# Smaller buffers and fewer streamed bytes in a recurrent attention over memory: casts into the operand tiles, softmax in PSUM, one output buffer

## The chip, the cores and the metric

The kernel runs on one core of a Trainium2 chip, in one launch. The metric is device time in microseconds: the median of several executions. The profile is of one further execution; its times are in microseconds from the start of its span unless marked ns. PE is TensorE (matmuls; PEld its weight loads), DVE is VectorE, ACT is ScalarE, POOL is GpSimd, SP is SyncE, which issues most DMAs.

## The reference, cut to what matters

The output is two results side by side. Part A is a sliding, dilated attention over x (2048 x 640). Part B, which the change touches, is a recurrence over 64 segments of 32 rows. The 8 memory rows that one segment gives are the memory of the next, so segments can't overlap freely.

```python
for s in range(n_seg):                        # 64 segments, seg_len 32, M = 8, H = 32, Dh = 192
    xs = x[:, s * seg_len:(s + 1) * seg_len, :]
    h = jnp.concatenate([mem, xs], axis=1)    # 40 rows of 640
    q, k, v = (jnp.einsum('btd,dhe->bhte', h, W) for W in (Wq, Wk, Wv))
    scores = jnp.where(mask, jnp.einsum('bhqe,bhke->bhqk', q, k) * scale, -1e9)
    o = jnp.einsum('bhqk,bhke->bhqe', softmax(scores), v)
    o = jnp.einsum('bhte,hed->btd', o, Wo)
    mem = o[:, :M, :]
    outs.append(o[:, M:, :])
```

## The kernel before, in words

**Order of the whole.** Part A comes first; while it runs, the weights of part B that stay in SBUF are loaded, and those that don't are copied into DRAM tiles of their own (`copy_streamed`, L347). Then 64 segments follow (`segment`, L695), and at the end one projection over all segments of the rows that no later segment needs (`project_late`, L776).

**Weights.** Each of q, k, v is cut into four groups of heads of five pieces (`dc`), 384 KB each; Wo into 24 pieces of 320 KB. `STREAMED` (L285) names the pieces that are fetched in every segment from their DRAM copy into one of 7 rotating buffers (`fetch`, L434; SP's queue). All others are resident.

**A segment** runs group by group (g = 0 to 3), in an order written out by hand as tokens: `FIRST` for segment 0, `ORDER` (L297) for the others. PE, DVE, ACT and SP execute their instructions in just that order; each engine takes from a token what is its own. The tokens:

- `q.g k.g v.g` (L504): projections, 32-row tiles, into PSUM `acc` (3 buffers). Once in four segments a group's k and v are also made for the 8 late rows of four segments (`ahead`); q's come one segment early (`ql`).
- `e.k1` (L546): the cast of `acc` into an SBUF tile `sb`, on the engine that `EVACUATE` names (S is ACT, V is DVE; the first letter is for `ahead`, the second for the segment's own). `T.k1` (L549): DVE turns `sb` in 32 x 32 blocks into QT or KT (L522), of which there is one each, and POOL fills the 8 late columns from a kept block `Lb` (L538, L541, L554).
- `S.g` (L573): the scores into a PSUM bank (`px`, 4 in all). `sb.g` (L580) scales and masks them into an SBUF tile `t1`, `mx` (L587), `sub` (L591, and ACT's exp, L592), `send` (L596, L597, L606): the rest of the softmax, into P.
- `tp.g` (L613), `PT.g` (L619): P is turned through PE and spread. `ve.g` (L562): v is kept in `Vst`. `mix.g` (L632): P times V into two banks.
- `ot.g` (L638): two copies, on the engines that `HEADS` names, bring the two halves of the mix into OT (L640). POOL then copies the 8 late columns of OT into OL (L641), which has two halves by g, and issues the DMA that stores OL in DRAM as `late_o` (L642). OT is one tile: `out.g` (L660) reads it as PE's weights.
- `part`, `join`: the two sums of groups 0 to 2 are joined. `last` (L682): group 3's share of the output, into Z. It reads the first half of OT in its first 24 matmuls, the second in the other 24.
- `close` (L685): DVE adds Z and `part` into XS (L687), turns it (L482) and copies the 8 memory rows into HX (L690), the operand of the next segment's first projection. POOL issues the DMAs of the output (L692).

Of the kernel before, what the change touches and what calls it, by code (L numbers as in the profile page):

```python
# [7 lines left out]
FP32 = mybir.dt.float32  # L8
# [15 lines left out]
def part_a(ctx, tc, A_x, A_wqkv, A_wo, out, ident, emit_loads):  # L24
# [241 lines left out]
    with tc.manual_schedule(engines={mybir.EngineType.PE, mybir.EngineType.DVE, mybir.EngineType.Activation}):  # L266
# [4 lines left out]
        for b in range(-1, n_blk):  # L271
# [13 lines left out]
STREAMED = {"q": ((), (), (), ()), "k": ((0, 1, 4), (3,), (0, 3, 4), (0, 1, 3)), "v": ((0, 3), (0, 3), (0, 4), (2, 4)),  # L285
            "o": (9, 11, 14, 16, 20, 23)}
SLOT = 1536
RENEW = {0: ("k0", "v2"), 1: ("k1", "v3"), 2: ("k2", "v0"), 3: ("k3", "v1")}
BLOCKS = 18
FIRST = """  # L290
    q.0 e.q0 T.q0 k.0 e.k0 T.k0 q.1 e.q1 k.1 S.0 sb.0 T.q1 e.k1 mx.0 sub.0 T.k1 send.0 q.2 e.q2 v.0 ve.0
    S.1 sb.1 tp.0 PT.0 T.q2 k.2 e.k2 T.k2 mx.1 sub.1 mix.0 ot.0 v.1 ve.1 send.1 S.2 sb.2 out.0.0 out.0.1
# [24 lines left out]
def part_b(ctx, tc, B_x, B_mem0, B_Wq, B_Wk, B_Wv, B_Wo, out, ident, n_seg, pre, nbuf, mid):  # L317
# [26 lines left out]

    copied = {}

    def copy_streamed():  # L347

        for m, g in need:
            for u in pieces(m, g):  # L350
                if streamed(u):
                    copied[u] = dpool.tile([128, unit_cols(u)], BF16, name="wcopy_%s%d_%d" % u)[:]
                    nc.sync.dma_start(two_rows(copied[u], u), unit_src(u))
# [4 lines left out]
    for m, g in need:  # L358
        resident += [u for u in pieces(m, g) if not streamed(u)]
    res, wait = {}, set()  # L360

    def place_resident(pool, units):
        for u in units:
            res[u] = pool.tile([128, unit_cols(u)], BF16, name="wres_%s%d_%d" % u)[:]

    def load_resident(units):
        for u in units:
            nc.sync.dma_start(two_rows(res[u], u), unit_src(u))

    n_pre, used = 0, 0  # L370
    while n_pre < len(resident) and used < pre:
        used += 2 * unit_cols(resident[n_pre])
        n_pre += 1
# [48 lines left out]
    qk_sb = pool("b_qk", bufs=3)  # L422
# [11 lines left out]
    def fetch(u):  # L434
        t = wstream.tile([128, SLOT], BF16, tag="ws")
        nc.sync.dma_start(t[:, 0:unit_cols(u)], copied[u])
        return t[:, 0:unit_cols(u)]

    def get_unit(u):
        if u in fetched:  # L440
            return fetched.pop(u)
        if u in res:
            if u in wait:
                wait.remove(u)
                load_resident([u])
            return res[u]
        return fetch(u)
# [15 lines left out]
    OT = cpool.tile([128, 12, L], BF16, name="OT")  # L463
    OL = cpool.tile([128, 2, M, 12], BF16, name="OL")
# [33 lines left out]
    def columns(w, m, j):  # L498

        if m == "v":  # L500
            return w[:, 384 * j:384 * j + 384].rearrange("p (f n) -> p f n", n=32)
        return w.rearrange("p (f j n) -> p j f n", j=4, n=32)[:, j]

    def project32(Xs, m, g, part=slice(0, 5), ps=None):  # L504

        if ps is None:
            ps = [ps_acc.tile([128, 384], FP32, tag="acc", name=f"acc{n}") for n in range(len(Xs))]
        for dc in range(5)[part]:
            w = get_unit((m, g, dc))
            for n, X in enumerate(Xs):  # L510
                for j in range(4):
                    nc.tensor.matmul(ps[n][32 * j:32 * j + 32].rearrange("p (f n) -> p f n", n=32), lhsT=X[:, dc, :],  # L512
                                     rhs=columns(w, m, j), start=(dc == 0), stop=(dc == 4), tile_position=(0, 32 * j))
        return ps
# [6 lines left out]
    def turn(dst, sb):  # L521
        nc.vector.transpose(dst, sb[:].rearrange("p (f n) -> p f n", n=32))  # L522
# [8 lines left out]
    def turn_late(sb, m, g, s, start):  # L531

        lt = sb[:].rearrange("p (f n) -> p f n", n=32)
        turn(lt, sb)
        for t in range(start, next_start(m, g, start)):
            rows = lt[:, :, M * (t % 4):M * (t % 4) + M]
            if t == s:
                nc.gpsimd.tensor_copy(columns_of(m, 32, L), rows)  # L538
            else:
                late[m, g, t] = free.pop(0)  # L540
                nc.gpsimd.tensor_copy(late[m, g, t][:], rows)  # L541
# [4 lines left out]
    def evacuate(ps, copies):  # L546
        return [to_sb(p, c) for p, c in zip(ps, copies[2 - len(ps):])]

    def turn_and_fill(s, m, g, sbs):  # L549
        if renewed(s, m, g):  # L550
            turn_late(sbs[0], m, g, s, s)
        else:
            b = late.pop((m, g, s))
            nc.gpsimd.tensor_copy(columns_of(m, 32, L), b[:])  # L554
            free.append(b)
        turn(columns_of(m, 0, 32), sbs[-1])
# [21 lines left out]
    def soft_begin(Sps):  # L578
        t1 = one.tile([128, 4, L], FP32, tag="t1")
        nc.vector.scalar_tensor_tensor(out=t1[:], in0=Sps, scalar=scale,  # L580
                                       in1=mask[:].unsqueeze(1).to_broadcast([128, 4, L]),
                                       op0=ALU.mult, op1=ALU.add)
        return t1
# [54 lines left out]
    def keep_mix(s, g, ps, copies):  # L638
        for r, copy in enumerate(copies):
            copy(OT[:, 6 * r:6 * r + 6].rearrange("p c n -> p (c n)"), ps[r][:, 0:6 * L])  # L640
        nc.gpsimd.tensor_copy(OL[:, g % 2].rearrange("p n c -> p c n"), OT[:, :, 32:L])  # L641
        nc.gpsimd.dma_start(late_o[s // 4][:, g, s % 4], OL[:, g % 2].rearrange("p n c -> p (n c)"))  # L642
# [5 lines left out]

    def wide(w, r, gv):
        return w[:, 640 * r:640 * r + 640].rearrange("p (b g c) -> p g b c", b=2, g=2)[:, gv]  # L650

    def project_out(Y, g, pairs=range(6)):
        for a in pairs:
            i = 6 * g + a
            w = get_unit(("o", i, 0))
            for r in range(2):
                c = 2 * a + r
                for gv in range(2):
                    t = 32 * (2 * r + gv)
                    nc.tensor.matmul(Y[t:t + 32].rearrange("p (b c) -> p b c", b=2),  # L660
                                     lhsT=OT[:, slot(c), 0:32], rhs=wide(w, r, gv),
                                     start=(i == 0), stop=(i == 17), tile_position=(0, t))

    def join_begin(Y):
        part = one.tile([128, 4, L], FP32, tag="t1", name="part")[:].rearrange("p a n -> p (a n)")
        for b in range(2):
            S_(part[64 * b:64 * b + 64], Y[64:128, 160 * b:160 * b + 160])
        return part
# [5 lines left out]

    def project_last(Y):
        for a in range(6):
            w = get_unit(("o", 18 + a, 0))
            for r in range(2):
                c = 2 * a + r
                for j in range(4):  # L680
                    n = 640 * r + 160 * j
                    nc.tensor.matmul(Y[32 * j:32 * j + 32], lhsT=OT[:, slot(c), 0:32], rhs=w[:, n:n + 160],  # L682
                                     start=(c == 0), stop=(c == 11), tile_position=(0, 32 * j))

    def close(s, Y, part):  # L685
        Ysb, T = XS[:], Vst[:, 0:160]
        nc.vector.tensor_tensor(Ysb, Y, part, op=ALU.add)  # L687
        if s + 1 < n_seg:
            turn32(T.rearrange("p (k n) -> p k n", n=SEG), Ysb)
            nc.vector.tensor_copy(HX[:, 0, :, 0:M], T.rearrange("p (k n) -> p k n", n=SEG)[:, :, 0:M])  # L690
# [4 lines left out]
    def segment(s):  # L695
# [12 lines left out]
        def step(name, *at):  # L708
# [3 lines left out]
            elif name == "e":  # L712
                m = at[0][0]
                got["sb", m, g] = evacuate(got.pop((m, g)), [engine[c] for c in EVACUATE[at[0]]])
            elif name == "T":
                m = at[0][0]
                turn_and_fill(s, m, g, got.pop(("sb", m, g)))
# [31 lines left out]
            elif name == "join":  # L749
                join_end(got["Y"], got["part"])  # L750
            elif name == "tx":
# [8 lines left out]
            elif name == "close":  # L760
                close(s, got["Z"], got["part"])
            elif name == "Tql":
                if not last:
                    gl = (s + 1) % 4
                    turn_late(got["sbl"], "q", gl, s, s + 1)
# [10 lines left out]
    def project_late():  # L776
# [8 lines left out]
        def add(m, i, w, first, final):  # L785
            for r in range(2):
                c = (2 * i + r) % 12
                for gv in range(2):
                    for j in range(4):
                        nc.tensor.matmul(sums[2 * m + gv][32 * j:32 * j + 32, 0:320], lhsT=O[4 * m + j][:, i // 6, :, slot(c)],  # L790
                                         rhs=w[:, 640 * r + 320 * gv:640 * r + 320 * gv + 320],
                                         start=first and r == 0, stop=final and r == 1, tile_position=(0, 32 * j))

        def store(m):
            rows = res[DEAD[16 + m]][:, 0:640]
            for gv, copy in ((0, S_), (1, V_)):
                copy(rows[:, 320 * gv:320 * gv + 320], sums[2 * m + gv][:, 0:320])
# [118 lines left out]
```

## Time and profile before

| | |
|---|---|
| Median of 3 runs | 1902.7 us (1901.57 to 1906.56) |
| The profiled execution's own time | 1902.95 us |
| Its span | 1901.2 us, 91723 instructions |
| Mean granted PE clock | 0.988 |
| DMA, whole span | 649.28 MB, mean 342 GB/s |

A row of the costliest groups has line, engine and operation, `out<-in` by tile names, shapes, a count, then after the bar the busy time in us, the mean ns of one, and the engine's idle time before them with what ended it. A row of the waits says who stood waiting for whom: us in all, times, the longest. A row of DMA issues ends with the median us from issue to landing. A row of a stretch has for each engine its busy us and count, in the order PE, PEld, DVE, ACT, POOL, then the granted clock, the DMA engines' share of the time and GB/s. In the chain in order of time and in the timeline, the first number is the start and the second how long it took.

### The profile page before, as it was taken

The numbers are of one execution on the slowest core, as the hardware profiler recorded it, in microseconds if no ns is written. First come the engines' busy times: TensorE is split into PE (matmuls) and PEld (weight loads), VectorE is DVE, ScalarE is ACT, GpSimd is POOL, SyncE is SP. The second block draws the span as 40 slices with busy tenths as digits, with TensorE's granted clock in tenths as the row PEclk, the third lists the DMA queues.
The fourth block names the chain that finished last, engine by engine and source line by source line (L and its number), as shares of the span: only waits on it lengthen the run. The fifth ranks groups of instructions, "written<-read, shape, count | busy, mean of one in ns | idle before, by whom it ended". The sixth has DMA issues, their size and how long they took to land.

```text
span 1901.2 us, 91723 instructions
## 1 busy us (share of the span) xinstructions
PE 1655.8 (87%) x39286; PEld 1042.3 (55%) x39286; DVE 1236.2 (65%) x3495; ACT 695.6 (37%) x1806; POOL 690.6 (36%) x1864
## 2 busy tenths in 40 slices
PE   8997898888888888888888888888889888888888
PEld 5565555555555555555555555555555555555558
DVE  4886676676666666676666676666667676666630
ACT  3453343333333333333333333333333333333320
POOL 3001344344433343433434433334444343443420
PEclk9999999999999999999999999999999999999999
DMA  9927999999999999999999999999999999999991
GB/s 328 318 71 254 329 380 361 376 371 371 352 362 356 359 362 354 350 374 348 355 365 352 362 368 336 359 363 369 370 385 372 356 372 348 349 355 342 372 381 52
DMA packets 286356, 649.28 MB, mean 342 GB/s; under 512 B 61140, under 2 KB 76946, under 8 KB 285948
## 3 DMA queue, kind: packets, MB, share of 16 engines
q1 hardware_dynamic: 267036, 630.01, 91.5%
q0 software_dynamic: 18400, 13.08, 2.2%
q8 instruction: 308, 5.05, 1.0%
q14 instruction: 100, 0.82, 0.1%
q10 hardware_dynamic: 512, 0.33, 0.1%
HBM read 629.10 MB, written 23.24 MB: 343 GB/s over the span
## 4 chain that ended last, share of the span: by engine, by line
PE 57%; DMA 26%; DVE 7%; issue 5%; ACT 2%; POOL 1%; SPq 0%; ACTq 0%; POOLq 0%; DVEq 0%
PE acc L512 30%; DMA t<-wcopy_k 10%; DMA t<-wcopy_o 7%; PE Y L660 7%; DMA t<-wcopy_v 7%; PE px L632 5%; PE px L573 4%; PE pq L95 3%; PE px L682 3%; PE px L790 1%; PE px L613 1%; DVE prod L151 1%; PE po L161 1%; ACT OT L640 1%; PE acc L790 1%
## 5 line engine op out<-in xcount | busy, mean ns | idle before, releaser
L512 PEld LDWEIGHTS <-HX 128*32 128x32 bf16 x19380 | 495.1, 97 | 443.8 <-issue 140.3
L512 PE MATMUL acc<-t,HX 128*32 128x384 bf16 x5812 | 434.0, 332 | 55.1 <-DMA t<-wcopy_k 21.1
L512 PE MATMUL acc<-wres_q,HX 128*32 128x384 bf16 x6460 | 331.8, 329 | 79.4 <-DVE HX L690 67.3
L518 ACT CAST sb<-acc 128x384 bf16<-128x384 f32 x484 | 228.2, 476 | 448.3 <-PE acc L512 381.1
L512 PE MATMUL acc<-wres_v,HX 128*32 128x384 bf16 x3876 | 242.7, 330 | 3.8 <-issue 3.8
L641 POOL COPY OL<-OT 128x96 bf16<-128x96 bf16 x256 | 160.9, 629 | 213.4 <-ACT OT L640 147.0
L554 POOL COPY QT<-Lb 128x96 bf16<-128x96 bf16 x252 | 68.8, 273 | 453.6 <-PE px L573 444.4
L562 ACT CAST Vst<-acc 128x384 bf16<-128x384 f32 x256 | 123.7, 483 | 283.2 <-PE px L632 205.4
L660 PE MATMUL Y<-wres_o,OT 128*32 128x320 bf16 x3584 | 203.3, 303 | 22.8 <-ACT OT L640 14.7
L512 PE MATMUL acc<-wres_k,HX 128*32 128x384 bf16 x3232 | 207.7, 331 | 7.7 <-issue 7.4
L522 DVE STREAM_TRANSPOSE QT<-sb 128x384 bf16<-128x384 bf16 x256 | 143.9, 562 | 78.7 <-ACT sb L518 78.7
L640 ACT CAST OT<-px 128x240 bf16<-128x240 f32 x448 | 143.9, 366 | 111.4 <-PE px L632 109.7
L660 PEld LDWEIGHTS <-OT 128*32 128x32 bf16 x4608 | 118.9, 96 | 97.4 <-issue 37.7
L619 DVE TENSOR_TENSOR PT<-px,own 128x320 bf16<-128x320 f32 x256 | 124.8, 487 | 72.5 <-PE px L613 70.7
L642 POOL DMA_DIRECT2D late_o<-OL x256 | 139.4, 545 | 81.5 <-POOL OL L641 74.5
L522 DVE STREAM_TRANSPOSE KT<-sb 128x384 bf16<-128x384 bf16 x256 | 144.4, 564 | 23.4 <-ACT sb L518 21.7
L573 PEld LDWEIGHTS <-QT 64*64 64x64 bf16 (+1 forms) x4096 | 106.8, 109 | 83.8 <-issue 53.2
L592 ACT ACTIVATE t<-t 128x160 f32<-128x160 f32 x256 | 86.4, 338 | 170.4 <-DVE t L591 168.3
L573 PE MATMUL px<-KT,QT 64*64 64x40 bf16 (+1 forms) x4096 | 138.3, 189 | 11.9 <-DVE KT L522 3.9
L692 POOL DMA_DIRECT2D out_dram<-XS x256 | 129.2, 512 | 15.3 <-DVE XS L687 7.9
L518 DVE CAST sb<-acc 128x384 bf16<-128x384 f32 x162 | 87.2, 547 | 58.7 <-PE acc L512 43.1
L632 PE MATMUL px<-PT,Vst 64*128 64x80 bf16 (+1 forms) x2048 | 122.7, 212 | 1.8 <-issue 1.5
(96 smaller groups left out, 2188.3 us busy)
## 6 DMA issues: line engine op xcount, KB each, us to landing
t<-wcopy_k SPq DMA_DIRECT2D x640, 384.0 KB, 6.0
t<-wcopy_v SPq DMA_DIRECT2D x512, 384.0 KB, 6.1
t<-wcopy_o SPq DMA_DIRECT2D x396, 320.0 KB, 5.6
wres_q<-in_B_Wq_dram SPq DMA_DIRECT2D x20, 384.0 KB, 7.8
late_o<-OL POOLq DMA_DIRECT2D x256, 24.0 KB, 5.3
wres_q<-late_o SPq DMA_DIRECT2D x16, 384.0 KB, 7.4
wres_o<-in_B_Wo_dram SPq DMA_DIRECT2D x18, 320.0 KB, 7.2
wres_v<-in_B_Wv_dram SPq DMA_DIRECT2D x12, 384.0 KB, 7.9
```

The lines of the kernel that those rows point to most:

```text
L512: nc.tensor.matmul(ps[n][32 * j:32 * j + 32].rearrange("p (f n) -> p f n", n=32), lhsT=X[:, dc, :], rhs=columns(w, m, j), start=(dc == 0), ...
L518: copy(sb[:], p[:])
L522: nc.vector.transpose(dst, sb[:].rearrange("p (f n) -> p f n", n=32))
L562: S_(Vst[:], ps[-1][:])
L573: nc.tensor.matmul(Sps[64 * h:64 * h + 64, a, :], lhsT=QT[k0:k1, L * f:L * f + 64], rhs=KT[k0:k1, f, :], start=(outer == 0 and a == 0), st ...
L619: nc.vector.tensor_tensor(PT[:], pt.rearrange("p l (h n) -> p (l h) n", h=2)[:, :, 0:L].unsqueeze(2) .to_broadcast([128, 4, 2, L]), own[:] ...
L632: nc.tensor.matmul(ps[r][lo:hi, 2 * L * k:2 * L * k + 2 * L], lhsT=V[64 * r:64 * r + 64, col:col + hi - lo], rhs=PT[64 * r:64 * r + 64, 2 ...
L640: copy(OT[:, 6 * r:6 * r + 6].rearrange("p c n -> p (c n)"), ps[r][:, 0:6 * L])
L641: nc.gpsimd.tensor_copy(OL[:, g % 2].rearrange("p n c -> p c n"), OT[:, :, 32:L])
L642: nc.gpsimd.dma_start(late_o[s // 4][:, g, s % 4], OL[:, g % 2].rearrange("p n c -> p (n c)"))
L660: nc.tensor.matmul(Y[t:t + 32].rearrange("p (b c) -> p b c", b=2), lhsT=OT[:, slot(c), 0:32], rhs=wide(w, r, gv), start=(i == 0), stop=(i ...
L692: nc.gpsimd.dma_start(out2[SEG * s:SEG * s + SEG - M, Dm + 160 * j:Dm + 160 * j + 160], Ysb[32 * j + M:32 * j + SEG])
```

## The change

1. **Streaming.** k, v and o have other streamed pieces, and three pieces (`PARTS`) are streamed in part: a piece is cut into four quarters, the first 2 or 3 are fetched, the others stay resident. Wo's quarters are kept in the column order of its two sums.
2. **Buffers.** `qk_sb` has 1 buffer instead of 3, `t1` is gone, there are 16 kept blocks instead of 18, OT holds 32 columns instead of 40, OL has one half instead of two.
3. **Casts.** `e` casts the segment's own q and k straight into QT and KT; `T` turns them there, in place. Only the `ahead` part still goes through `sb`. For k0 the kept copies come after T.k1.
4. **Softmax** scales, masks, subtracts and takes exp in the scores' PSUM bank.
5. **OT and OL.** After each of the two copies into OT, the same engine copies the late columns from PSUM into OL. POOL only issues the DMA.
6. **The last sum.** join also turns `part` (`turn_part`); close turns Z from PSUM and adds the turned 8 rows into HX, and only then adds the full rows for the output. `part` and its turned form lie in QT and KT, the turned Z in Vst.
7. `ORDER`, `FIRST`, `EVACUATE` and `HEADS` are others; the copy of `ahead` v (LV) moves from ACT to DVE.

The diff, cut to its core:

```diff
-STREAMED = {"q": ((), (), (), ()), "k": ((0, 1, 4), (3,), (0, 3, 4), (0, 1, 3)), "v": ((0, 3), (0, 3), (0, 4), (2, 4)),
-            "o": (9, 11, 14, 16, 20, 23)}
+STREAMED = {"q": ((), (), (), ()), "k": ((0, 4), (0, 3), (1, 4), (0, 2, 3)), "v": ((0, 2, 4), (2, 4), (0, 3), (2, 4)),
+            "o": (4, 10, 13, 15, 21, 23)}
+PARTS = {("o", 10, 0): 3, ("v", 1, 2): 2, ("v", 2, 3): 3}
-BLOCKS = 18
+BLOCKS = 16
 ORDER = """
-    q.0 e.q0 k.0 T.q0 e.k0 T.k0 k.1 q.1 S.0 e.k1 k.2 e.q1 q.2 sb.0 T.k1 T.q1 S.1 e.k2 mx.0 v.0 sub.0
-    send.0 e.q2 T.q2 q.3 tp.0 sb.1 ve.0 v.1 mx.1 T.k2 sub.1 S.2 PT.0 mix.0 send.1 e.q3 tp.1 ve.1 sb.2
-    k.3 ot.0 mx.2 out.0.0 v.2 PT.1 out.0.1 T.q3 sub.2 e.k3 T.k3 send.2 mix.1 S.3 ve.2 v.3 ot.1 sb.3 mx.3
-    sub.3 tp.2 PT.2 out.1.0 out.1.1 mix.2 send.3 tp.3 PT.3 tx ot.2 ve.3 out.2.0 out.2.1 mix.3 part ql
-    ot.3 eql last join close Tql
+    q.0 k.0 e.q0 e.k0 T.q0 T.k0 q.1 k.1 S.0 e.q1 v.0 e.k1 sb.0 mx.0 T.q1 sub.0 T.k1 q.2 ve.0 S.1 send.0
+    sb.1 mx.1 e.q2 sub.1 k.2 e.k2 tp.0 T.q2 PT.0 send.1 v.1 q.3 T.k2 mix.0 ve.1 tp.1 PT.1 S.2 ot.0 sb.2
+    k.3 e.q3 mx.2 T.q3 mix.1 out.0.0 e.k3 out.0.1 sub.2 T.k3 v.2 send.2 tp.2 ot.1 S.3 ve.2 sb.3 v.3 mx.3
+    out.1.0 sub.3 PT.2 mix.2 out.1.1 send.3 tp.3 ve.3 ot.2 out.2.0 out.2.1 PT.3 mix.3 tx part ql ot.3
+    join eql last close Tql
 """
-EVACUATE = {"k0": "VS", "k1": "VV", "k2": "SS", "k3": "SV", "q0": "SS", "q1": "VS", "q2": "SS", "q3": "SS"}
-HEADS = ("SS", "VS", "SS", "SS")
+EVACUATE = {"k0": "SV", "k1": "SS", "k2": "SS", "k3": "VS", "q0": "SV", "q1": "SS", "q2": "SS", "q3": "VS"}
+HEADS = ("VS", "SS", "SV", "SS")
...
-    qk_sb = pool("b_qk", bufs=3)
+    qk_sb = pool("b_qk", bufs=1)
...
-    OT = cpool.tile([128, 12, L], BF16, name="OT")
-    OL = cpool.tile([128, 2, M, 12], BF16, name="OL")
+    OT = cpool.tile([128, 12, 32], BF16, name="OT")
+    OL = cpool.tile([128, M, 12], BF16, name="OL")
...
-    def evacuate(ps, copies):
-        return [to_sb(p, c) for p, c in zip(ps, copies[2 - len(ps):])]
+    def evacuate(m, ps, copies):
+        sb = to_sb(ps[0], copies[0]) if len(ps) > 1 else None
+        copies[1](columns_of(m, 0, 32), ps[-1][:].rearrange("p (f n) -> p f n", n=32))
+        return sb
...
-            S_(LV[g][:], ps[0][:])
+            V_(LV[g][:], ps[0][:])
...
-        t1 = one.tile([128, 4, L], FP32, tag="t1")
-        nc.vector.scalar_tensor_tensor(out=t1[:], in0=Sps, scalar=scale,
+        nc.vector.scalar_tensor_tensor(out=Sps, in0=Sps, scalar=scale,
...
         for r, copy in enumerate(copies):
-            copy(OT[:, 6 * r:6 * r + 6].rearrange("p c n -> p (c n)"), ps[r][:, 0:6 * L])
-        nc.gpsimd.tensor_copy(OL[:, g % 2].rearrange("p n c -> p c n"), OT[:, :, 32:L])
-        nc.gpsimd.dma_start(late_o[s // 4][:, g, s % 4], OL[:, g % 2].rearrange("p n c -> p (n c)"))
+            o = ps[r][:, 0:6 * L].rearrange("p (c n) -> p c n", n=L)
+            copy(OT[:, 6 * r:6 * r + 6], o[:, :, 0:32])
+            copy(OL[:, :, 6 * r:6 * r + 6].rearrange("p n c -> p c n"), o[:, :, 32:L])
+        nc.gpsimd.dma_start(late_o[s // 4][:, g, s % 4], OL[:].rearrange("p n c -> p (n c)"))
...
+    def turn_part(part):
+        partT = KT[:].rearrange("p f n -> p (f n)")[:, 0:320].bitcast(FP32).rearrange("p (k n) -> p k n", n=SEG)
+        turn32(partT, part)
+        return partT
...
-    def close(s, Y, part):
-        Ysb, T = XS[:], Vst[:, 0:160]
+    def close(s, Y, part, partT):
+        Ysb, T = XS[:], Vst[:, 0:320].bitcast(FP32).rearrange("p (k n) -> p k n", n=SEG)
+        if s + 1 < n_seg:
+            turn32(T, Y)
+            nc.vector.tensor_tensor(HX[:, 0, :, 0:M], T[:, :, 0:M], partT[:, :, 0:M], op=ALU.add)
         nc.vector.tensor_tensor(Ysb, Y, part, op=ALU.add)
-        if s + 1 < n_seg:
-            turn32(T.rearrange("p (k n) -> p k n", n=SEG), Ysb)
-            nc.vector.tensor_copy(HX[:, 0, :, 0:M], T.rearrange("p (k n) -> p k n", n=SEG)[:, :, 0:M])
...
             elif name == "T":
                 m = at[0][0]
-                turn_and_fill(s, m, g, got.pop(("sb", m, g)))
+                keep = fill_late(s, m, g, got.pop(("sb", m, g)))
+                turn_in_place(columns_of(m, 0, 32))
```

More of the change, by code (lines that the diff above doesn't have):

```diff
@@ L350, in copy_streamed @@
             for u in pieces(m, g):
-                if streamed(u):
+                if u in PARTS:
+                    copied[u] = dpool.tile([128, stream_cols(u)], BF16, name="wcopy_%s%d_%d" % u)[:]
+                    load_quarters(copied[u], u, range(PARTS[u]))
+                elif streamed(u):
                     copied[u] = dpool.tile([128, unit_cols(u)], BF16, name="wcopy_%s%d_%d" % u)[:]
@@ L358, in part_b @@
     for m, g in need:
-        resident += [u for u in pieces(m, g) if not streamed(u)]
+        resident += [u for u in pieces(m, g) if not streamed(u) or u in PARTS]
     res, wait = {}, set()
@@ L533, in turn_late, with keep, fill_late @@
         lt = sb[:].rearrange("p (f n) -> p f n", n=32)
[L534 to L539, printed above, removed]
+        turn_in_place(lt)
+        rows = lambda t: lt[:, :, M * (t % 4):M * (t % 4) + M]
+        if start == s:
+            nc.gpsimd.tensor_copy(columns_of(m, 32, L), rows(s))
+        def keep():
+            for t in range(max(start, s + 1), next_start(m, g, start)):
                 late[m, g, t] = free.pop(0)
-                nc.gpsimd.tensor_copy(late[m, g, t][:], rows)
+                nc.gpsimd.tensor_copy(late[m, g, t][:], rows(t))
+        return keep
     def project_qk(s, m, g):
         return project32([ahead, main] if renewed(s, m, g) else [main], m, g)
-    def evacuate(ps, copies):
-        return [to_sb(p, c) for p, c in zip(ps, copies[2 - len(ps):])]
[L549 to L556, printed above, removed]
+    def evacuate(m, ps, copies):
+        sb = to_sb(ps[0], copies[0]) if len(ps) > 1 else None
+        copies[1](columns_of(m, 0, 32), ps[-1][:].rearrange("p (f n) -> p f n", n=32))
+        return sb
+    def fill_late(s, m, g, sb):
+        if sb is not None:
+            return turn_late(sb, m, g, s, s)
+        b = late.pop((m, g, s))
+        nc.gpsimd.tensor_copy(columns_of(m, 32, L), b[:])
+        free.append(b)
     def values(s, g):
@@ L660, in project_out @@
                     nc.tensor.matmul(Y[t:t + 32].rearrange("p (b c) -> p b c", b=2),
[L661 removed]
+                                     lhsT=OT[:, slot(c), 0:32], rhs=quarter(w, ("o", i, 0), 2 * r + gv),
                                      start=(i == 0), stop=(i == 17), tile_position=(0, t))
     def join_begin(Y):
[L665 removed]
+        part = QT[:, 0:320].bitcast(FP32)
         for b in range(2):
@@ L750, in step @@
                 join_end(got["Y"], got["part"])
+                got["partT"] = None if last else turn_part(got["part"])
             elif name == "tx":
```

93 lines of the change are left out of this document (63 added, 30 removed).

## The prediction

> **What bounds the kernel now.** I read the page's busy shares first, then the steady part by itself (the stretch from the first to the last hand-over between segments), the hand-over's own rows, and the waits.
>
> ```profile
> PE 1655.8 (87%) x39286; PEld 1042.3 (55%) x39286; DVE 1236.2 (65%) x3495; ACT 695.6 (37%) x1806; POOL 690.6 (36%) x1864
> ...
> PE 57%; DMA 26%; DVE 7%; issue 5%; ACT 2%; POOL 1%; SPq 0%; ACTq 0%; POOLq 0%; DVEq 0%
> ```
> ```profile
> 216.80:1810.50 1593.70, 1390.72 (x34472) 857.22 (x34472) 1074.77 (x3256) 588.84 (x1581) 639.37 (x1735) 0.99 0.99 362
> ```
> ```profile
> L690 DVE COPY HX<-Vst x63: 174/175/582, 216.6 to 1810.3; 128x40 bf16<-128x40 bf16 x63
> ```
> ```profile
> PE acc L512 <- DVE HX L690: 67.3, 63, 1.4
> POOL OL L641 <- DMA late_o<-OL: 63.0, 37, 2.7
> ...
> PE acc L512 <- DMA t<-wcopy_k: 21.1, 45, 1.7
> ...
> PE acc L512 <- DMA t<-wcopy_v: 15.6, 30, 6.4
> ...
> PE Y L660 <- DMA t<-wcopy_o: 11.1, 25, 1.1
> ```
>
> L690 runs once a segment, 63 times from 216.6 to 1810.3: 62 distances of 25.70 us. In that stretch the DMA engines are busy 0.99 of the time at 362 GB/s and PE 1390.72 of 1593.70 us, 22.4 us a segment. So DMA and PE are both near their limits. PE's direct waits for streamed weights are small all the same, 21.1 + 15.6 + 11.1 = 47.8 us, 0.77 a segment: that is all PE can win from fewer bytes as long as the rest of its order stays. The hand-over costs it 67.3/63 = 1.07.
>
> Keep the second wait in mind: today POOL, which nobody waits for, stands 63.0 us for `late_o` transfers, although OL has two halves.
>
> **The bytes.** Streamed a segment before: 10 pieces of k and 8 of v at 384 KB, 6 of o at 320 KB, 8832 KB. After: k 9 x 384; v seven whole, one half (192), one three quarters (288); o five whole and one of 240: 3456 + 3168 + 1840 = 8464 KB. That is 4.2% less, at 0.99 x 25.70 us of DMA time worth 1.06 us if time goes by bytes. PE can take at most its 0.77. The room for it comes from the smaller buffers.
>
> **The hand-over.**
>
> ```profile
> L522 DVE STREAM_TRANSPOSE KT<-sb 128x384 bf16<-128x384 bf16 x256 | 144.4, 564 | 23.4 <-ACT sb L518 21.7
> ...
> L619 DVE TENSOR_TENSOR PT<-px,own 128x320 bf16<-128x320 f32 x256 | 124.8, 487 | 72.5 <-PE px L613 70.7
> ...
> L592 ACT ACTIVATE t<-t 128x160 f32<-128x160 f32 x256 | 86.4, 338 | 170.4 <-DVE t L591 168.3
> ...
> L596 DVE TENSOR_REDUCE sm<-t 128x4 f32<-128x160 f32 x256 | 78.5, 307 | 44.4 <-ACT t L592 40.9
> ...
> L606 DVE TENSOR_TENSOR P<-t,sm 128x128 bf16<-128x128 f32 x256 | 75.5, 295 | 8.8
> ...
> L606 DVE TENSOR_TENSOR P<-t,sm 128x32 bf16<-128x32 f32 x256 | 48.6, 190 | 0.0
> ...
> L597 DVE RECIPROCAL sm<-sm 128x4 f32<-128x4 f32 x256 | 45.5, 178 | 8.8
> ...
> L482 DVE STREAM_TRANSPOSE Vst<-XS 128x160 bf16<-128x160 bf16 x63 | 22.3, 355 | 2.2
> L687 DVE TENSOR_TENSOR XS<-px,part 128x160 bf16<-128x160 f32 x64 | 20.8, 324 | 72.3 <-PE px L682 72.3
> ...
> L126 DVE TENSOR_REDUCE mx<-lg 128x64 f32<-128x512 f32 x8 | 5.5, 691 | 15.1 <-PE lg L118 15.0
> ...
> L137 DVE TENSOR_TENSOR P<-ex,sm 128x512 bf16<-128x512 f32 x8 | 5.5, 691 | 0.3
> ```
>
> Today it is L687, L482, L690: 0.324 + 0.355 + 0.175 = 0.85 us. After: a turn of 160 f32 columns from PSUM and a sum of 40 columns. No f32 turn is in the trace: at least the 0.355 of the bf16 one, at most twice that; the sum 0.18 to 0.32 (L690, L687). So between a gain of 0.3 and a loss of 0.2; I take a gain of 0.2, nearest to a turn at the same columns. The wide sum moves behind the hand-over, and the second turn (of `part`) goes into join, beside `ql` and `last`.
>
> **Softmax in PSUM.** The same instructions with other operands. L126 reads 512 f32 columns from PSUM, L137 as many from SBUF, both 691 ns: I take nothing. No DVE or ACT row here rewrites PSUM at this size; the ends are 0 and a tenth of each 0.31 us step. By the Trainium skill, "VectorE: DVE Perf Modes", section on the TRN2 errata, a PSUM source costs some 62 cycles (65 ns) more per instruction; the two equal rows do not bear that out.
>
> **Cast into QT and KT.** The turns stay (0.56 us), but a cast now writes a tile that the scores of the group before still read, so it waits for them. Between S.0 and S.1 the chain is cast, sb, mx, turn, sub, cast, turn, with five DVE steps (3 x 0.31 + 2 x 0.56) and a cast ahead, about 2.4 us; PE has v.0 and q.2 there, 1.9. In the same way tp.2 waits for sub.2, T.k3 and send.2. I charge 0.5 us a segment in all (0 if POOL and the order hide it, 1.0 if both stand in full).
>
> **OL: one buffer, written by ACT and DVE.** Gone are POOL's 0.63 us copies. Each of the two copies of OT is now followed on its own engine by one into OL, and the DMA that reads OL must have landed before the next group's first copy writes there. What waits is no longer POOL but ACT (ot.0 to ot.3) and DVE (ot.0, ot.2), in the order written out.
>
> ```profile
> t<-wcopy_k SPq DMA_DIRECT2D x640, 384.0 KB, 6.0
> ...
> late_o<-OL POOLq DMA_DIRECT2D x256, 24.0 KB, 5.3
> ```
> ```profile
> DMA to landing us min/median/max: 3.0/5.3/7.8
> ```
> ```profile
> DMA to landing us min/median/max: 2.0/3.8/9.2
> ```
> ```profile
> 745.44 0.55 POOL L642 DMA_DIRECT2D late_o<-OL  x1 [0.30 <-POOL OL L641]
> ```
> ```profile
> 747.41 0.62 ACT L640 CAST OT<-px 128x240 bf16<-128x240 f32 x2 [1.86 <-PE px L632]
> ...
> 748.92 0.59 ACT L667 COPY part<-Y 64x160 f32<-64x160 f32 x2
> 749.53 0.62 ACT L640 CAST OT<-px 128x240 bf16<-128x240 f32 x2
> ```
> ```profile
> 747.83 1.00 PE Y L660 x24
> 748.83 0.47 PE px L632 x16
> 749.30 0.93 PE acc L512 x20
> 750.23 0.86 PE px L682 x48
> ...
> 759.29 0.47 PE px L573 x16
> ...
> 763.21 0.22 PE px L613 x2
> ```
>
> The first landing row is that of `late_o` (3.0 least, 5.3 median), the second that of part A's `ob`, whose least, 2.0, fell where DMA was nearly idle. In the segment shown ot.2 ends at 748.03 and ot.3 starts at 749.53, 1.5 us later. The transfer starts 0.30 us after OL is written and takes L. After its first OT copy (about 0.35) ot.3 would write OL 1.85 us after ot.2's end, but may only at 0.30 + L: a wait of **L - 1.55**, 3.75 us at the median, 1.45 at the least of `late_o`, 0.45 at 2.0. **Behind it on ACT** stands the second half of OT, and for that waits the second half of `last`, which ends the segment. PE's cover is `ql` (0.93) and half of `last` (0.43).
>
> The wait also passes from group to group. With PE's pieces above (a projection 0.93, scores 0.47, mix 0.47, out 1.00, tp 0.22), an OL copy at 0.2 (the bounds are 0.175, L690, and POOL's 0.63 for twice the columns), and t = 0 at the end of mix.0:
>
> - ot.0 has written OL at 1.55; transfer at 1.85.
> - ot.1 may not touch OT before out.0.1 is done (3.1) and stands behind the exp of group 2; it wants OL at 3.85.
> - ot.2 wants it after out.1.1 and send.3, near 8.7. It holds ACT and, as its second half is on V, DVE, where PT.3 stands behind it and so mix.3.
> - ot.3 as above.
>
> With L = 4.0 for the first two: OL free at 5.85, ot.1 done at 6.6, OL free again at 10.9, PT.3 at 11.1 to 11.6, mix.3 at 11.7 where it could have started at 10.0: 1.7 us late. With L = 3.0 for the third, sent at 11.4: ot.3 gets OL at 14.4, OT's second half is there at 15.0, and PE wanted it at 13.7: 1.3. **Together 3.0 us a segment.** The same walk gives 0.3 with L = 2.0 throughout, 1.4 with 3.0, 7.9 with 5.3.
>
> The choice of L is the weak place. 5.3 was measured with DMA busy 0.99. If PE stands 3 us a segment, 8.67 MB in about 28 us is some 310 GB/s, and in the last wait all seven buffers are filled, so the queue runs empty. I take 4.0, 4.0, 3.0, between the loaded and the idle rows.
>
> **Sum a segment:** OL +3.0, casts +0.5, weight waits -0.77 (all gone, as PE is the later one), hand-over -0.2: +2.5. Over 64 segments +160 us on the profiled execution's 1902.95 (0.25 us from the median of 1902.7): **2063 us**, 28.2 a segment. Part A, the first loads (368 KB more resident, into a stretch where DMA idles) and the last projection stay within 2 us.
>
> **Rivals.**
>
> - *The waits on OL are covered* and the bytes decide. For it: DMA at 0.99 today, and L was down to 2.0 where DMA idled. Against: 37 waits of POOL with twice the buffers. Casts half hidden: 0.3 + 0.25 - 0.77 - 0.2 is -0.4; with nothing left of OL's wait, -0.7 or, by the bytes, -1.06: 1835 to 1880, 1865 as its middle. By the Trainium skill, "DMA: Bandwidth & Descriptors", section on the anatomy of a SWDGE DMA, such a transfer takes 2.0 us and its bytes over 436 GB/s, 2.06 for 24 KB; by that L this rival would hold. The median of 256 rows is 5.3, so the trace does not agree under load. Chance 0.20.
> - *L stays at 5.3* since the queue fills again after each wait: +7.9 + 0.5 - 0.97, 7.4 a segment, 2370; anything over 2200 I count here. Against: bytes a segment fall while it grows longer. Chance 0.10.
> - *A draw*: short waits on OL (1.4 at L = 3.0, less what stalls for the next instructions took anyway) and casts near 0 eat what the bytes give: 1897 to 1909. Chance 0.04.
>
> My own case, 1909 to 2200, has 0.66. The point from which the sign turns: PE's added stalls above 0.97 us a segment, which is an L of about 2.6 with the casts hidden.
>
> **Chances.** A change within 0.3% can't be told from none here. Faster 0.20, same 0.04, slower 0.76. For 8 in 10 the range takes in the slow case and most of the fast one and leaves out the long L and the ends: 1850 to 2200. The likeliest case's own range is 1930 to 2200.
>
> **What would show it.** In the waits: ACT (OL copies) waiting for DMA `late_o`, 2 to 4 us at a time, three a segment; PE at `last` (Z) waiting for ACT OT, and at mix waiting for DVE PT; DMA's share well under 0.99; `late_o` landing in 3 to 4.5; L690's place at 27 to 30 us a segment. Wrong if ACT's waits on `late_o` are short or PE does not wait at `last`; then the time is the bytes' and lies near 1865. The hand-over is wrong if PE's wait on HX grows; the casts, if S.1 and tp.2 don't wait.

## The result, and the profile after

The changed kernel takes **2381.2 us** (median of 4 runs, 2364.62 to 2388.35) against 1904.6 us (4 runs): a ratio of 1.249 [1.244, 1.254], 477 us more. The forecast of 2063 had the sign right and the size far too small; the time lies above the whole range. The profiled execution's own time is 2364.62 us.

The page of the changed kernel, its span, busy times and clock, ACT's copies into OL, and the group of PE's matmuls that stands the longest:

```profile
span 2362.8 us, 92077 instructions
...
PE 1829.6 (77%) x39286; PEld 1097.2 (46%) x39286; DVE 1318.8 (56%) x3801; ACT 714.0 (30%) x2075; POOL 526.9 (22%) x1608
...
PEclk9998898888898888988988889888888888988889
...
L681 ACT CAST OL<-px 128x48 bf16<-128x48 f32 x384 | 144.9, 377 | 455.4 <-DMA late_o<-OL 455.4
...
L723 PE MATMUL px<-t,OT 128*32 128x160 bf16 x1024 | 53.8, 304 | 220.4 <-ACT OT L680 220.4
```

PE runs the same 39286 matmuls, but is busy 174 us longer, and its clock row has 8s in most slices, where before all were 9s. ACT, idle most of the time before, now stands 455.4 us for the transfers that read OL. Next the hand-over's row and the steady stretch of the changed kernel (columns as before; granted clock, DMA share and GB/s at the end):

```profile
L731 DVE TENSOR_TENSOR HX<-Vst,KT x63: 199/199/201, 223.7 to 2270.1; 128x40 bf16<-128x40 f32 x63
```
```profile
223.90:2270.30 2046.40, 1563.61 (x34472) 912.27 (x34472) 1153.56 (x3549) 607.57 (x1845) 481.54 (x1488) 0.88 0.80 270
```

A segment is (2270.1 - 223.7)/62 = 33.0 us long, 7.3 more than 25.7. PE is busy 1563.61/62 = 25.2 of it (before 22.4) and stands 7.8 (before 3.3). The waits of the changed kernel say where:

```profile
POOL late_o L682 <- ACT OL L681: 711.3, 177, 7.3
ACT OL L681 <- DMA late_o<-OL: 455.4, 147, 6.0
...
PE px L723 <- ACT OT L680: 220.9, 65, 5.6
...
PE px L613 <- issue: 124.1, 60, 4.3
...
PE acc L549 <- DVE HX L731: 43.6, 63, 0.7
...
PE acc L549 <- DMA t<-wcopy_v: 23.3, 25, 10.7
...
PE acc L549 <- DMA t<-wcopy_k: 13.1, 26, 0.9
...
PE px L671 <- DVE PT L658: 10.1, 14, 1.8
```

Over 63 segments that is, for PE, 3.5 us each at `last` (L723), 2.0 at scores (L613), 0.69 at the hand-over (1.07 before), 0.58 for streamed k and v, 0.16 at mix for PT. The other short gaps make up the rest. So of the 7.3 us a segment, about 4.5 are standing and 2.8 are the same matmuls running longer.

**One segment end, followed through.** The timeline of the changed kernel, one segment, engine by engine. First ACT:

```profile
967.63 0.37 ACT L681 CAST OL<-px 128x48 bf16<-128x48 f32 x1 [1.55 <-DMA late_o<-OL]
...
973.93 0.32 ACT L680 CAST OT<-px 128x192 bf16<-128x192 f32 x1 [0.44 <-PE px L671]
979.23 0.37 ACT L681 CAST OL<-px 128x48 bf16<-128x48 f32 x1 [4.99 <-DMA late_o<-OL]
979.59 0.32 ACT L680 CAST OT<-px 128x192 bf16<-128x192 f32 x1
```
POOL, which issues the transfer of group 2:
```profile
973.47 0.54 POOL L682 DMA_DIRECT2D late_o<-OL  x1 [1.80 <-ACT OL L681]
```
PE in the same stretch:
```profile
968.09 0.54 PE L613 MATMUL px<-KT,QT 64*64 64x40 bf16 x16 [0.55 <-issue]
...
974.61 0.59 PE L723 MATMUL px<-wres_o,OT 128*32 128x160 bf16 x24
979.96 0.46 PE L723 MATMUL px<-t,OT 128*32 128x160 bf16 x8 [4.76 <-ACT OT L680]
...
981.65 1.79 PE L549 MATMUL acc<-wres_q,HX 128*32 128x384 bf16 x20 [0.70 <-DVE HX L731]
```
And two short stretches of it, the stop and what follows:
```profile
978.00:979.90 1.90, 0.00 (x0) 0.00 (x0) 0.00 (x0) 0.67 (x4) 0.00 (x0) 0.64 0.04 14
979.90:983.40 3.50, 2.74 (x48) 1.60 (x52) 1.34 (x4) 0.60 (x3) 1.75 (x4) 0.50 0.56 176
```

Read it backwards from 979.96. PE restarts when ACT has copied the second half of OT (979.59 + 0.32). That copy stands behind ACT's copy of the first half's late columns into OL, which waited 4.99 us for group 2's transfer, issued only at 973.47 since group 2's own copies had waited for group 1's transfer. Nothing else is late: from 978.0 to 979.9 PE, DVE and POOL do nothing, and the DMA engines are 0.04 busy, as all buffers are full; in SP's own waits the fetch (L473) stands for PE's matmuls of `last` to free one, 63 times:

```profile
SPq L473 <- PE px L723: 348.6, 63, 7.8
```
After the stop the granted clock is 0.50, and the first 20 matmuls of the next segment take 1.79 us. In the kernel before, its timeline at a hand-over, they took 1.00:

```profile
752.09 1.00 PE L512 MATMUL acc<-wres_q,HX 128*32 128x384 bf16 x20 [1.03 <-DVE HX L690]
```

The stop at L613 is the same wait by another route. S.3 starts at 968.09, 0.09 us after ACT's first OL copy of group 1 ended (967.63 + 0.37), and 58 of the 60 waits in the row above end 0.10 us after an OL copy does. The profile says "issue" as it shows no releaser; in the trace, PE's queue stands just ahead of S.3 for the semaphore that ACT counts up, whose one new count is that copy's. So it is the copy that S.3 waits for. Why it must is argued: the only things of one kind that the two touch are PSUM banks, so S.3 most likely needs the bank of mix.1 that this copy reads.

### The profile page after: what moved, and what is told of

Its sections match the earlier page's. It is cut to its first block, busy times and chain, and to the rows that moved or that the text cites. A ratio compares the mean times of both kernels' runs of the same rounds, so it can differ in the third digit from the quotient of the medians.

```text
span 2362.8 us, 92077 instructions
## 1 busy us (share of the span) xinstructions
PE 1829.6 (77%) x39286; PEld 1097.2 (46%) x39286; DVE 1318.8 (56%) x3801; ACT 714.0 (30%) x2075; POOL 526.9 (22%) x1608
## 5 line engine op out<-in xcount | busy, mean ns | idle before, releaser
L549 PE MATMUL acc<-wres_q,HX 128*32 128x384 bf16 x6460 | 383.6, 375 | 44.1 <-DVE HX L731 43.6
L681 ACT CAST OL<-px 128x48 bf16<-128x48 f32 x384 | 144.9, 377 | 455.4 <-DMA late_o<-OL 455.4
L613 PE MATMUL px<-KT,QT 64*64 64x40 bf16 (+1 forms) x4096 | 141.4, 191 | 146.7 <-issue 124.1
L549 PE MATMUL acc<-wres_k,HX 128*32 128x384 bf16 x3552 | 252.8, 366 | 2.2 <-issue 2.2
L619 DVE SCALAR_TENSOR_TENSOR px<-px,mask 128x160 f32<-128x160 f32 x256 | 93.5, 365 | 274.2 <-PE px L613 158.7
L723 PE MATMUL px<-t,OT 128*32 128x160 bf16 x1024 | 53.8, 304 | 220.4 <-ACT OT L680 220.4
L588 ACT CAST QT<-acc 128x384 bf16<-128x384 f32 x192 | 98.6, 514 | 411.3 <-PE px L613 410.5
L613 PEld LDWEIGHTS <-QT 64*64 64x64 bf16 (+1 forms) x4096 | 111.4, 111 | 215.2 <-issue 173.1
L723 PEld LDWEIGHTS <-OT 128*32 128x32 bf16 x3072 | 69.0, 110 | 241.6 <-ACT OT L680 234.6
L697 PEld LDWEIGHTS <-OT 128*32 128x32 bf16 x4608 | 115.5, 104 | 71.0 <-ACT OT L680 19.6
L559 DVE STREAM_TRANSPOSE KT<-KT 128x384 bf16<-128x384 bf16 x256 | 141.3, 552 | 12.6 <-ACT KT L588 12.5
L559 DVE STREAM_TRANSPOSE QT<-QT 128x384 bf16<-128x384 bf16 x256 | 145.3, 567 | 0.0
L680 ACT CAST OT<-px 128x192 bf16<-128x192 f32 x384 | 137.1, 357 | 16.1 <-PE Y L697 9.4
```

What stands on the lines that cost most here:

```text
L559: nc.vector.transpose(t, t)
L588: copies[1](columns_of(m, 0, 32), ps[-1][:].rearrange("p (f n) -> p f n", n=32))
L613: nc.tensor.matmul(Sps[64 * h:64 * h + 64, a, :], lhsT=QT[k0:k1, L * f:L * f + 64], rhs=KT[k0:k1, f, :], start=(outer == 0 and a == 0), st ...
L619: nc.vector.scalar_tensor_tensor(out=Sps, in0=Sps, scalar=scale, in1=mask[:].unsqueeze(1).to_broadcast([128, 4, L]), op0=ALU.mult, op1=ALU ...
L680: copy(OT[:, 6 * r:6 * r + 6], o[:, :, 0:32])
L681: copy(OL[:, :, 6 * r:6 * r + 6].rearrange("p n c -> p c n"), o[:, :, 32:L])
```

## The experiments

Each kernel is timed against the kernel before on the same chip: 1902.45 us for those named e1 to e4, 1901.42 for e5 to e8, 1906.02 for e9 to e12.

**Is it the one buffer?** The theory: all of the loss comes from OL having one half. The rivals: the chain of casts into QT and KT, the new order, the fewer blocks.

```diff
-PARTS = {("o", 10, 0): 3, ("v", 1, 2): 2, ("v", 2, 3): 3}
+PARTS = {("v", 1, 2): 2, ("v", 2, 3): 3}
-    OL = cpool.tile([128, M, 12], BF16, name="OL")
+    OL = cpool.tile([128, 2, M, 12], BF16, name="OL")
...
+            copy(OL[:, g % 2, :, 6 * r:6 * r + 6].rearrange("p n c -> p c n"), o[:, :, 32:L])
```
This is `e1_ol_two`; `e2_ol_four` has four and the index g. The room for OL comes from streaming Wo's piece 10 whole again (8544 KB a segment).

> The changed kernel with OL in two halves by g, as before; ACT and DVE still write it. To make room in SBUF, o piece 10 is streamed whole (8544 KB a segment instead of 8464). Theory A (the one OL buffer, with what stands behind its copies on ACT and DVE, makes the time; the low PE clock follows from PE's long idle times): the granted clock is back above 0.96, PE's wait for ACT OT at last is under 1 us a segment, the time 1870 to 1930 us. Theory B (the casts into the single QT and KT, the softmax that holds its PSUM banks and the new order make it): clock near 0.89 and time above 2200.

> The changed kernel with four OL tiles, one for each g, o piece 10 streamed whole (8544 KB a segment). Theory A: no wait on late_o at all, clock as before (0.98), 1850 to 1900 us, at or under the kernel before; what the time then stands above the bytes' 1865 is the price of casts and order. Theory B: above 2200, like the first run of this call.

Measured: two halves 1903.22 us, 1.000 [0.997, 1.003]; four 1898.69 us, 0.998 [0.995, 1.002]. The whole loss is gone. In the waits of the kernel with two halves, what was 455.4 us:

```profile
ACT OL L681 <- DMA late_o<-OL: 1.9, 3, 0.8
```
And its steady stretch, with the clock back at 0.99 and the PE busy time of before:
```profile
223.10:1810.00 1586.90, 1389.66 (x34472) 849.61 (x34472) 1152.11 (x3551) 609.71 (x1845) 481.52 (x1488) 0.99 0.98 352
```

The other way round, `e3_before_ol_one` takes one half away from the kernel before, where POOL writes OL:
```diff
-    OL = cpool.tile([128, 2, M, 12], BF16, name="OL")
+    OL = cpool.tile([128, 1, M, 12], BF16, name="OL")
...
+        nc.gpsimd.tensor_copy(OL[:, 0].rearrange("p n c -> p c n"), OT[:, :, 32:L])
```

> The kernel before with one OL half instead of two, POOL still copying OT into OL. Theory A in its narrow form (it matters that ACT and DVE are the ones that wait): POOL waits much longer for late_o, but since OT is freed only when POOL has read it, ot.3 is held up in part: 1930 to 2150. In its wide form (any single OL chains the groups through the DMA's landing): 2150 to 2400, clock under 0.92. If POOL's waits are free: under 1920.

Measured: 2225.25 us, 1.169 [1.165, 1.173]. Its waits:
```profile
POOL OL L641 <- DMA late_o<-OL: 501.1, 158, 6.3
...
ACT OT L640 <- POOL OL L641: 309.7, 98, 5.8
...
PE px L682 <- ACT OT L640: 190.9, 62, 5.5
```
Before, the waits for POOL's copies into OL came to 0.3 us outside POOL; with one half POOL passes the transfer's time on to ACT (which may not rewrite OT until POOL has read it) and ACT to PE. So one half costs 323 us even where POOL writes it. The further 154 us of the changed kernel most likely go with the copy's new place, on the engine that PE waits for; that is argued, as no run moved the copy alone at one half. With two halves, that place is free of loss in the new order (`e1_ol_two`).

**Does the order of the copies matter, and what is the clock's share?** `e4_ot_first` copies both halves of OT first, then both of OL:
```diff
             copy(OT[:, 6 * r:6 * r + 6], o[:, :, 0:32])
+        for r, copy in enumerate(copies):
+            o = ps[r][:, 0:6 * L].rearrange("p (c n) -> p c n", n=L)
             copy(OL[:, :, 6 * r:6 * r + 6].rearrange("p n c -> p c n"), o[:, :, 32:L])
```

> The changed kernel, one OL buffer, but in ot both copies into OT stand ahead of both copies into OL. Theory A: PE's wait for ACT OT at last goes (3.6 us a segment to under 0.5), the waits on late_o stay on ACT and DVE, PT.3 stays late and the banks of the mix stay held; 2050 to 2250 us, clock between 0.90 and 0.97. Theory B: within 2% of the changed kernel's 2381.

Measured: 2241.38 us, 1.177 [1.172, 1.182]; 140 us of the 477 come back. PE's wait at `last` is gone, but ACT waits as long as before, and now PE stands elsewhere behind it:
```profile
ACT OL L683 <- DMA late_o<-OL: 457.4, 150, 6.4
...
PE px L613 <- issue: 157.7, 63, 4.0
...
PE acc L549 <- ACT sb L555: 100.5, 73, 4.0
...
PE px L613 <- POOL QT L595: 67.1, 46, 4.7
```
These three rows of PE hold 325.3 us; in the changed kernel the same three held 124.1 + 3.2 + 1.6 = 128.9. A wait that an engine moves behind its own work reaches what is queued next on it, here the casts into `sb`, QT and KT.

`e5_warm` keeps the changed kernel and lets PE multiply 50 identity blocks, whose result nobody reads, between the halves of `last`, where it stands anyway:
```diff
+        D = ps_acc.tile([128, 384], FP32, tag="acc", name="warm")
         for a in range(6):
             w = get_unit(("o", 18 + a, 0))
+            if a == 3:
+                for _ in range(WARM):
+                    nc.tensor.matmul(D[:, 0:128], lhsT=ident, rhs=ident, start=True, stop=True)
```

> The changed kernel with 50 matmuls of the identity (128x128, into an acc buffer that nobody reads) between the halves of last, where PE stands 3.5 us a segment: the waits stay, only PE is not idle in them. If the low granted clock is a price of its own that follows the idle time, q.0 after the hand-over goes from 1.79 back to 1.0 us, the clock rises to 0.93 to 0.96 (the stop at S.3 stays), and the time falls by 1 to 2 us a segment: 2250 to 2320. If the low clock costs nothing beside the waits, since ACT and the DMA set the pace anyway: 2365 to 2395.

Measured: 2301.44 us, 1.209 [1.202, 1.216], 80 us less than the changed kernel, with ACT's waits unchanged. Its timeline at one segment end:
```profile
980.86 2.96 PE L724 MATMUL warm<-ident 128*128 128x128 bf16 x50
985.18 0.32 PE L728 MATMUL px<-t,OT 128*32 128x160 bf16 x8 [1.35 <-ACT OT L681]
...
986.47 1.00 PE L550 MATMUL acc<-wres_q,HX 128*32 128x384 bf16 x20 [0.69 <-DVE HX L736]
```
The 20 matmuls after the hand-over take 1.00 us in place of 1.79, and the 8 of `last` 0.32 in place of 0.46. So some 80 us is the price of the half clock behind that one stop, as far as other waits didn't take up the gain; the stop at S.3 (122.3 us in this kernel) and the clock behind it weren't treated.

**Are the bytes worth anything?** `e6_before_less_bytes` is the kernel before with Wo's piece 23 not streamed; the resident piece 22 stands in for it:
```diff
-            "o": (9, 11, 14, 16, 20, 23)}
+            "o": (9, 11, 14, 16, 20)}
+GONE, INSTEAD = ("o", 23, 0), ("o", 22, 0)
...
+        u = INSTEAD if u == GONE else u
```
`e9_handover_less_bytes` and `e10_ol_four_less_bytes` do the same to the kernel with the new hand-over (`e8_before_handover`, below) and to `e2_ol_four`.

> The kernel before with o piece 23 not streamed: o piece 22, which is resident, stands in for it, so one piece of the output projection is computed with other weights, and 8512 KB a segment are streamed instead of 8832 (3.6% less). If the bytes are the limit: 0.9 us a segment less, 1840 to 1860. If only PE's waits for weights can go (0.77 a segment): 1855 to 1885. If PE's own chain is the limit and those waits only move elsewhere: 1890 to 1903.

> The kernel before with the new last sum (1888.4 alone), and o piece 23 not streamed: piece 22 stands in for it, so one piece of the output projection is computed with other weights; 8512 KB a segment instead of 8832. With the hand-over shorter, DMA's share was 0.999. If the bytes are the limit now: 1840 to 1860. If, as without the new last sum (1907.6 against 1901.4), fewer bytes give nothing in this order: 1880 to 1900.

> The four-OL kernel (1898.7) with o piece 23 not streamed, piece 22 standing in for it, so one piece of the output projection is computed with other weights: 8224 KB a segment instead of 8544. If bytes count in the new order, as the 45 us between 8544 and 8832 KB suggest: 1850 to 1870. If those 45 us came from where the streamed pieces stand in the new order, not from their number: 1890 to 1905.

Measured: 1907.6 us, 1.002 [0.999, 1.005]; 1894.61 us, 0.995 [0.992, 0.998], where the same kernel with all bytes has 0.994 [0.990, 0.997]; 1901.19 us, 0.999 [0.995, 1.002], beside 0.998 for `e2_ol_four`. 320 KB of 8.5 to 8.8 MB less does nothing, three times; `e6_before_less_bytes` came out even a little above the range for "nothing", 1890 to 1903. Its steady stretch is no shorter, and the DMA engines now have time left:
```profile
218.50:1821.70 1603.20, 1394.46 (x34472) 857.39 (x34472) 1074.13 (x3256) 588.41 (x1581) 639.09 (x1737) 0.99 0.97 347
```
In its waits, PE's for weights:
```profile
PE acc L514 <- DMA t<-wcopy_v: 21.9, 44, 7.2
...
PE acc L514 <- DMA t<-wcopy_k: 10.3, 24, 1.2
...
PE Y L662 <- DMA t<-wcopy_o: 9.9, 22, 1.3
```
42.1 us in all against 47.8 before. The bytes fall, these waits hardly do.

`e7_ol_four_streams_before` is `e2_ol_four` with the streamed pieces of before (`STREAMED` as before, `PARTS = {}`, 8832 KB).

> The four-OL kernel with the streamed pieces of the kernel before, no partial pieces, 8832 KB a segment instead of 8544. All else is that of the changed kernel. If the bytes are worth what they are in the kernel before's order (0.7 to 0.9 us a segment for 3.3%), it is 1935 to 1960, and casts and order cost those 2 to 3% against the kernel before. If the bytes are worth nothing here: 1890 to 1910, and the new order neither wins nor costs.

Measured: 1943.88 us, 1.021 [1.014, 1.028], 45 us more than `e2_ol_four` for 3.4% more bytes. That lies in the range which the expectation gave to bytes that count, but `e10_ol_four_less_bytes` then showed that fewer bytes gain nothing in this order either. One reason that fits is which pieces are fetched when, under an order they weren't chosen for. Another is that the bytes begin to count between 8544 and 8832 KB: both kernels move 352 to 353 GB/s in their steady stretch, and the stretch grows by the 3.4% of the bytes (1580.1 to 1635.9 us). It stays open: no run changed the places alone.

**The other parts one by one.** `e8_before_handover` is the kernel before with the new `close` and `turn_part` alone, and for them `join` ahead of `eql`:
```diff
-    ot.3 eql last join close Tql
+    ot.3 join eql last close Tql
...
+            turn32(T, Y)
+            nc.vector.tensor_tensor(HX[:, 0, :, 0:M], T[:, :, 0:M], partT[:, :, 0:M], op=ALU.add)
+        nc.vector.tensor_tensor(Ysb, Y, part, op=ALU.add)
```
`e11_handover_psum` adds the softmax in PSUM to it (`out=Sps` for `out=t1[:]`, `return Sps`). `e12_handover_ol_direct` adds instead the copies into OL from PSUM by ACT and DVE, with OL's two halves and OT at 32 columns.

> The kernel before with the changed kernel's last sum alone: part turned in join, Z turned from PSUM, the full rows added after (join stands ahead of eql in the order). PE's wait for HX falls from 1.07 to about 0.69 us a segment, as in the changed kernel. If that lies on the path: 1875 to 1885. If DMA sets the pace, PE waits for weights instead, by as much: 1897 to 1905.

> The kernel before with the new last sum and with the softmax in the scores' PSUM bank, in the old order. If PSUM operands cost nothing, as predicted, and the held banks stop nobody: 1880 to 1897. If the held banks stop PE (a mix or a tp waits for a bank): above 1900.

> The kernel before with the new last sum, and ACT and DVE writing OL from PSUM in place of POOL, into two halves. The added copies take 0.37 us each, four pairs a segment. If they lie beside other work: 1880 to 1897, and POOL's 0.63 us copies were no cost either. If they hold back OT's second half or the casts: 1900 to 1930.

Measured: the hand-over 1888.43 us, 0.994 [0.990, 0.997]; with the softmax in PSUM 1889.73, 0.993 [0.991, 0.996]; with OL written directly 1906.55, 1.002 [0.999, 1.005]. So **the hand-over alone is better than the kernel before**, by 13 us (the time lies between the two ranges expected); the softmax's place costs nothing; the direct copies, with OT at 32 columns, cost some 0.8%. In the waits of `e12_handover_ol_direct` stands the chain of the changed kernel in small:
```profile
ACT OL L642 <- DMA late_o<-OL: 31.0, 40, 2.2
...
PE px L688 <- ACT OT L641: 19.6, 28, 2.0
```
PE's wait at `last` for ACT's OT was 0.7 us in `e8_before_handover`; 0.8% is 15 us. This speaks for two halves being not quite enough in the old order, once ACT waits for the transfer itself. The steady stretch of `e8_before_handover`:
```profile
216.10:1795.20 1579.10, 1397.63 (x34472) 862.14 (x34472) 1107.69 (x3317) 588.26 (x1581) 642.34 (x1734) 0.99 1.00 365
```

The same bytes as before, in a stretch 14.6 us shorter, at 365 GB/s instead of 362: a DMA share of 0.99 still left this much room.

## Why the prediction was wrong in size, step by step

- **The OL term was mis-sized**, and this is the step that failed: +3.0 us a segment was charged, and it is 7.4, the 33.0 of the changed kernel less the 25.6 of `e1_ol_two` (1586.90/62). Its mechanism held: ACT waits for `late_o`, 4.99 us in the segment shown, PE for ACT's OT at `last`, the wait handed from group to group; `e1_ol_two` takes it all away. Three things were off.
  - **L.** 4.0, 4.0 and 3.0 were taken for the first three transfers; their means over the 64 segments of the changed kernel, from issue to landing, are 5.07, 3.18 and 4.70. The median of all, 4.0, is what was taken for two of them; where the short one falls was taken wrongly. The third is the costly one: the queue was expected to run empty there, but 3.8 weight fetches on average are issued in the 4 us before ot.2's transfer (1.9 before ot.1's), and in the segment shown the DMA engines are still busy behind it up to 978.0:

```profile
974.80:978.00 3.20, 0.40 (x24) 0.20 (x12) 0.10 (x1) 0.00 (x0) 0.00 (x0) 1.00 0.81 302
```
  With these three the prediction's own walk gives: OL free at 1.85 + 5.07 = 6.92, again at 6.92 + 0.75 + 0.3 + 3.18 = 11.15, mix.3 at 11.95 (1.95 late), the third transfer out at 11.65 and landed at 16.35, OT's second half at 16.95, wanted at 13.95 (3.0 late): 4.95 a segment. Measured were 3.5 + 2.0 + 0.16 = 5.7. (At L = 2.0 and 3.0 throughout, the steps as written give some 0 and 1.0, not 0.3 and 1.4; the forecast's sum doesn't use these two.)
  - **The place.** PT.3 was to be late by 1.7; it was late by 0.16. The wait came out at S.3 instead, which waits for ACT's OL copy and most likely for the bank that it frees. The prediction had listed who stands behind the waiting copy on ACT, but not who needs what that copy reads. An OL copy takes 0.37 us, for which 0.2 was taken.
  - **The clock.** A stop was charged at its own length. After it PE runs at half clock for a while, and PE's busy time grows by 2.8 us a segment. No term of the sum had this. `e5_warm` shows 80 us of it behind one of the two stops.
- **The rival at 2370**, which has nearly the measured time, isn't what happened: it wanted L at 5.3 and 7.9 us of stops. The median landing is 4.0 and the stops came to 5.7; the clock made up the rest, so that it comes so close is luck. (Its 7.4 a segment is 2377, not 2370.)
- **The bytes**, -0.77, were wrong: PE's waits for k and v are 36.4 us in the changed kernel where they were 36.7, and only those for o fell (11.1 to 2.0), in a segment that is 7.3 us longer anyway; three kernels with fewer bytes gained nothing. A DMA share of 0.99 was read as a limit of the rate. That PE waits for single pieces that are late and not for the sum of bytes fits these runs, but none of them moved a single piece to show it.
- **POOL, "which nobody waits for"**: that holds for its copies into OL alone. For the kept blocks that POOL writes (Lb, L541) ACT stood 53.5 us and DVE 15.0 in the kernel before. The forecast doesn't rest on it.
- **The hand-over**, -0.2, came out at -0.38 in its wait (1.07 to 0.69) and -13 us in `e8_before_handover`, or -0.2 a segment; that the time has just the charged size is in part luck. The two rows that the trace of before did not have:

```profile
L518 DVE STREAM_TRANSPOSE Vst<-px 128x160 f32<-128x160 f32 x63 | 22.0, 350 | 269.6 <-PE px L723 269.6
...
L731 DVE TENSOR_TENSOR HX<-Vst,KT 128x40 bf16<-128x40 f32 x63 | 12.6, 200 | 2.2
```
  0.350 + 0.200 = 0.55 us where 0.85 stood, 0.30 less. The turn from PSUM in f32 costs what the bf16 one from SBUF did (355 ns), the low end of the bounds.
- **Softmax in PSUM**, 0, was right: `e11_handover_psum` against `e8_before_handover` is 0.1% apart, within both intervals. The rows of the two agree, here the maximum from SBUF (`e8_before_handover`) and from PSUM (`e11_handover_psum`):

```profile
L587 DVE TENSOR_REDUCE mx<-t 128x4 f32<-128x160 f32 x256 | 79.1, 309 | 6.6
```
```profile
L586 DVE TENSOR_REDUCE mx<-px 128x4 f32<-128x160 f32 x256 | 80.5, 314 | 6.6
```
  The other DVE steps of the softmax moved by -10 to +9 ns. By the Trainium skill, "VectorE: DVE Perf Modes", section on the TRN2 errata, an instruction with a PSUM source should cost some 62 cycles (65 ns) more, an estimate from two columns of its table; these rows don't bear that out.
- **The casts**, +0.5, were not run alone. `e1_ol_two` holds them together with the new order and the new streaming, beside the parts of `e12_handover_ol_direct` and the softmax: 1.000 against 1.002, with intervals of 0.3% each way. +0.5 us a segment would be 1.7%: it isn't there unless the new order and streaming pay for it, which stays open. In the waits of `e1_ol_two` PE does stand for these casts, turns and fills, 13.6 us for ACT's QT, 11.3 for POOL's QT and 6.3 for DVE's KT, or 0.5 a segment.
- **The faster rival** (waits covered, 1865) asked for landings near 2 us; the third alone took 4.7. Even with the waits gone, `e1_ol_two` and `e2_ol_four` stand at before, not at 1865: the bytes brought nothing.

## What to carry to other kernels

When a change halves a buffer that a DMA reads, walk the loop with landing times of the loaded queue, and follow for each late instruction both what is queued behind it on its engine and what it frees for others (here, most likely, a PSUM bank). Price a stop of PE of several us at more than its length, for the clock after it: in the three kernels with one half of OL the same matmuls grew by 2.8, 2.3 and 1.6 us a segment (the changed kernel, `e3_before_ol_one`, `e4_ot_first`), beside 4.5, 2.9 and 3.7 of added standing. And before a change is made to save bytes, take one transfer out with a stand-in and see whether the time moves: a busy share near 1 didn't mean that it would.

## What the runs showed of the hardware

The clock gate, in numbers: with stops of 3.5 and 2.0 us in each 33-us segment the mean granted clock fell from 0.988 to 0.888, to 0.50 in the stretch after a stop, in 102 of 106 cases for 3.41 us or twice that, and the same 39286 matmuls took 1829.6 us in place of 1655.8. By the Trainium skill, "TensorE: Matmul & The Clock Gate", Part 1 on the clock gate, the clock goes to half after an idle window of about 3.4 us and back after a busy one, in windows that run freely; the lengths in the trace agree. What wasn't expected is that stops of 3.5 and 2.0 us in each loop cost so much, and that 3 us of useless matmuls in one of them win back 80 us.

The transfers from OL in the changed kernel:

```profile
DMA to landing us min/median/max: 1.8/4.0/6.7
```
24 KB land in 1.8 us at least, 4.0 at the median with the DMA engines 0.80 busy, where it was 5.3 at 0.99. The mean share doesn't tell a single one: in the same loop ot.1's take 3.18 us on average and ot.2's 4.70. What goes with it is the number of weight fetches issued in the 4 us before: with at most two of them the transfer takes 3.2 us on average (114 of 256), with four or five 5.0 (105).
